# Banded attention followed by a two-layer block: the four VectorE copies that build the attention masks stand in slot 10 of the loop and not in slot 1

## Chip, cores and metric

The kernel runs on one core of a Trainium2 chip. The metric is the device time of one execution in microseconds (us); less is better. The engines are named as in the profile: PE is TensorE (its weight loads are PEld), DVE is VectorE, ACT is ScalarE, POOL is GpSimd, SP is SyncE.

## What is computed

Attention with 8 batches, 8 heads, 576 positions and 64 dimensions a head, in which a position sees only those at most 32 away, and then a block of two matrix products with a smooth ReLU between them on the 4608 tokens of 512 features:

```python
scores = q @ k.T / 8 ; mask = |pos_i - pos_j| <= 32
attn   = softmax(where(mask, scores, -1e9))
x      = (attn @ v) with the heads side by side        # 4608 x 512
h      = x @ w_in                                      # 4608 x 2048
g      = h if h >= 1 ; 0 if h <= -1 ; (h + 1)**2 / 4 between
out    = g @ w_out                                     # 4608 x 512
```

## The kernel before

**Tiles.** Everything is done in bf16 on PE, with sums in fp32. Tokens go in groups of 256 (`TB`), 18 of them. The first product takes 8 pieces of 256 of the 2048 features for each group, so there are 144 of these steps. Each pass of the big loop (`a` from 0 to 151, called a **slot** here) makes one such step: 8 matmuls of line 463 into a PSUM tile `hp`, then a ReLU on ACT (line 467), a maximum on DVE (line 469) and a minimum with a product on DVE (line 470) that give a piece of `gT`. The tile `hp` has two PSUM banks to rotate through (in slots 6 and 7 one of another pool), and the maximum is the last to read it, so the matmuls of slot `a + 2` need the maximum of slot `a`.

The second product is cut in **quarters** (`quarter`, line 414): 4 matmuls with 4 of the 16 rows of `w_out`. From slot 16 on there is one quarter in a slot, for the group before; the eight quarters of the very first group of tokens are spread over slots 9 to 15 by a list written out by hand: `(9, 0), (11, 4), (12, 1), (13, 5), (13, 2), (14, 6), (15, 3), (15, 7)`. The first number is the slot. Quarters 3 and 7 take the last quarter of `w_out`.

**The attention beside it.** What the attention needs is put between these steps by the table `ev`, also by hand: transposes of q and k on PE with a copy out of PSUM (`tpose`, lines 178 to 181), scores (lines 218 and 243) with an exponential on ACT, the sums over the band (line 284), their reciprocal on ACT and the product that writes `xT` on DVE (lines 296 and 299). Whole numbers run before the slot's quarters, and halves such as 1.5 after them. In slots 1 and 1.5 the transposes of the second half of q and k of batch 0 are made. Each has two parts; the first part is copied out of PSUM by ACT and the second by DVE, and the second part of k uses the PSUM bank that the second part of q was in. From slot 2 to slot 16 all such copies are ACT's.

**The masks.** The band is applied in one of two ways. In slots before 14 a matmul with the identity adds a large negative bias to the scores (`add_mask`, line 197). From slot 14 on DVE multiplies the exponentials by `mask4` or `mask8` (line 192), two bf16 tiles of ones and zeros, 128x1024 and 128x384. They are made once, by four DVE copies that repeat a piece of `band`, two for each half of the partitions (line 475). The first multiplication with a mask comes in slot 19.

**Loads.** All inputs but the first q come by DMAs that POOL issues, in the order of the program: k and v of batch 0, the first quarter of `w_in`, the second half of q and k, the other twelve pieces of `w_in`, then q and k of batch 1 with the first part of `w_out`, two more parts of `w_out`, v of batch 1, and the second half of batch 1 with the last part of `w_out` as its first transfer. Each of POOL's DMAs waits, before it is issued, for the landing of the one that used the same of eight semaphores, so that at most eight are under way. Each engine takes its instructions in the order of the program, which is written by hand (`manual_schedule`).

Of the kernel before, what the change touches and what calls it, by code (L numbers as in the profile page):

```python
# [14 lines left out]
def kernel(  # L15
# [72 lines left out]
    def load_nat(b, t):  # L88
        src, dst, nm = ((q, qn, "qn"), (k, kn, "kn"))[t]
        x = dst[b] = nat.tile([128, NU, 2, D], BF, name=nm, tag=nm)  # L90
        for h in range(2):
            nc.gpsimd.dma_start(out=x[:, :, h], in_=src[b, NY * h:NY * h + NY].rearrange("y s d -> (y s) d")  # L92
                                .rearrange("(u p) d -> p u d", p=128))

    def load_v(b, n):
        if b not in vn:
            vn[b] = nat.tile([128, 2 * NC, 2, D], BF, name="vn", tag="vn", bufs=3)
        h, a = divmod(n, 2)
        y = NY * h + 2 * a
        nc.gpsimd.dma_start(out=vn[b][64 * a:64 * a + 64, :, h], in_=v[b, y:y + 2].rearrange("y s d -> (y s) d")  # L100
                            .rearrange("(c r) d -> r c d", r=64))
# [81 lines left out]
    def xpose(b, t):  # L183

        nc.sync.dma_start_transpose(out=qkT(b, t).rearrange("d (u p) -> d u p", p=128),
                                    in_=(qn, kn)[t][b].rearrange("p u h d -> p (u h d)"))
# [115 lines left out]
    def flush():  # L302
        while muls:
            muls.pop(0)()
# [93 lines left out]
    for b in range(LONG, B):  # L398
        a = sl[5 * (b - 1) - 7] - 17
# [7 lines left out]
    def quarter(x):  # L407

        tt, ff = divmod(x, 4)
        if tt not in op:  # L410
            op[tt] = ps_o.tile([128, DM], FP, name="op", tag="op"), []
        o, done = op[tt]
        for j in range(4 * ff, 4 * ff + 4):
            nc.tensor.matmul(o, gT[tt // 2][:, j, 128 * (tt % 2):128 * (tt % 2) + 128], w_out[:, j],  # L414
                             start=not done, stop=len(done) == 2 * NF - 1, skip_group_check=True)
            done.append(j)
        if len(done) == 2 * NF:
            osb = osp.tile([128, DM], FP, name="osb")
            A.copy(osb, o)  # L419
            nc.sync.dma_start(out=out[128 * tt:128 * tt + 128, :], in_=osb)  # L420

    def run(pos):
        todo = []
        for fn, *x in ev.get(pos, []):
            if fn is sums:
                todo.append(sums(*x))
            elif fn is tpose:
                part = x.pop()
                todo.append(tpose(*x, (A.copy, V.tensor_copy)[part if pos < 2 or pos > 16 else 0], tp1((ps_s, ps_n)[part])))
                if part:  # L430
                    while todo:
                        todo.pop(0)()
            elif fn is keep_warm:
                keep_warm(*x)
            else:
                pool = (x.pop(),) if x[-1] in (ps_s, ps_n, ps_o) else ()
                fn(*x, eng, *pool)
        for end in todo:
            end()

    for a in range(NF * NB + NF):
        t, f = divmod(a, NF)
        eng = None if a < 14 else V
        post = [x for n, x in quarters if n == a] if a < 2 * NF else [a - NF]
        for b, x in loads.get(a, []):
            if x < 2:
                load_nat(b, x)
            else:
                for n in range(4):
                    load_v(b, n)  # L450
        if a == 0 or a > 3:
            flush()
        if t < NB:
            if t not in gT:
                gT[t] = gtp.tile([128, 2 * NF, TB], BF, name="gT", tag="gT")
            r0 = TB * t % RING
            if a in (6, 7):
                hp = ps_o.tile([128, 2, TB], FP, name="hp", tag="op")
            else:
                hp = ps_h.tile([128, 2, TB], FP, name="hp", tag="hp")  # L460
            for j in range(2):
                for n, kk in enumerate((0, 2, 1, 3)):
                    nc.tensor.matmul(hp[:, j], w_in[:, kk, 256 * f + 128 * j:256 * f + 128 * j + 128],  # L463
                                     xT[:, kk, r0:r0 + TB], start=n == 0, stop=n == 3)

            rr = ewp.tile([128, 2, TB], FP, name="rr")
            A.activation(rr, hp, AF.Relu, scale=0.5, bias=0.5)  # L467
            mx = ewp.tile([128, 2, TB], FP, name="mx")
            V.tensor_max(mx, hp, rr)  # L469
            V.scalar_tensor_tensor(gT[t][:, 2 * f:2 * f + 2], rr, 1.0, mx, op0=ALU.min, op1=ALU.mult)  # L470
        flush()
        if a == 1:
            for h in range(2):
                for m, n, w in ((mask4, 8, 128), (mask8, 4, TAIL)):
                    V.tensor_copy(m[HD[h]].rearrange("p (n j) -> p n j", n=n), band[HD[h], 64 * h:64 * h + w]
                                  .rearrange("p (n j) -> p n j", n=1).to_broadcast([64, n, w]))
        run(a)
        for x in post:
            quarter(x)
        run(a + 0.5)  # L480
        for x in xps.get(a, []):
            xpose(*x)
# [30 lines left out]
```

The softmax here doesn't subtract the row's maximum and nothing guards it: scores larger than these inputs give would overflow.

## Time and profile before

| | |
|---|---|
| four runs | 320.50, 320.57, 321.77, 321.84 us; median 321.17 |
| the profiled execution | 320.5 us, of which the profile's span is 318.4 and 2.1 lie around it |
| PE busy | 305.7 us (96% of the span) |
| DVE busy | 248.9 us (78%) |
| ACT busy | 193.5 us (61%) |
| POOL busy | 88.7 us (28%) |
| granted TensorE clock | 0.998 of full speed |

The profile is of one execution. Times in it count from the start of the span. A row of the timeline has the start, the duration, the engine, the line, the operation, what is written and read with its size, the number of instructions merged in the row, and in brackets the idle time of the engine before it with what ended that. A DMA's row on POOL is the issue alone; the landing is later, and the trace has its time by the semaphore that it raises.

### The profile page before, as it was taken

How to read it: one execution, taken by the hardware profiler on the slowest of the kernel's cores; microseconds unless marked ns; L12 is line 12 of the kernel's file. 1: busy time of each engine (PE TensorE's matmuls, PEld its weight loads, DVE VectorE, ACT ScalarE, POOL GpSimd, SP SyncE). 2: the span in 40 equal slices, each digit the busy share in tenths (PEclk: the TensorE clock that was granted, in tenths of full speed). 3: DMA queues.
4: the chain of work that ended last, by engine and by line, in shares of the span. 5: the costliest groups of instructions: out<-in, count | busy, mean ns of one | idle time of the engine just before them, and what ended most of it. 6: DMA issues, size and time to landing. Idle time of an engine off the chain costs nothing.

```text
span 318.4 us, 8557 instructions
## 1 busy us (share of the span) xinstructions
PE 305.7 (96%) x3651; PEld 201.8 (63%) x3651; DVE 248.9 (78%) x390; ACT 193.5 (61%) x318; POOL 88.7 (28%) x121
## 2 busy tenths in 40 slices
PE   8968998999999999999999999999999999999995
PEld 3546665666666666666666666666666666667652
DVE  3278956787888888888888888888888888878760
ACT  3649656675775676666766666566676666554421
POOL 8795937896403706040502100000000000000000
PEclk9999999999999999999999999999999999999999
DMA  9999999999999999959991955005410010100111
GB/s 145 164 129 186 150 175 159 198 141 163 169 140 129 165 179 194 150 63 115 183 147 38 106 118 100 35 35 108 102 43 35 33 35 35 36 33 35 51 48 66
DMA packets 122661, 34.52 MB, mean 108 GB/s; under 512 B 108800, under 2 KB 117760, under 8 KB 122624
## 3 DMA queue, kind: packets, MB, share of 16 engines
q0 software_dynamic: 93760, 18.06, 73.0%
q1 hardware_dynamic: 28864, 15.93, 22.3%
q8 instruction: 28, 0.46, 0.6%
q14 instruction: 9, 0.07, 0.1%
HBM read 36.70 MB, written 9.44 MB: 145 GB/s over the span
## 4 chain that ended last, share of the span: by engine, by line
PE 79%; DMA 8%; POOL 7%; DVE 3%; ACT 2%; issue 1%; POOLq 0%; ACTq 0%
PE op L414 37%; PE hp L463 34%; DMA w_out<-in_moe_w_out_dram 6%; PE bb L284 5%; POOL w_in L104 3%; POOL vn L100 2%; DMA w_in<-in_moe_w_in_dram 2%; PE bb L218 2%; POOL kn L84 1%; DVE gT L470 1%; DVE mx L469 1%; PE tp L178 1%; ACT rr L467 1%; POOL w_out L108 0%; DVE pt L192 0%
## 5 line engine op out<-in xcount | busy, mean ns | idle before, releaser
L463 PE MATMUL hp<-xT,w_in 128*128 128x256 bf16 x1152 | 149.2, 273 | 0.7 <-DVE xT L299 0.5
L414 PE MATMUL op<-w_out,gT 128*128 128x512 bf16 x576 | 146.5, 380 | 1.3 <-DMA w_out<-in_moe_w_out_dram 1.3
L467 ACT ACTIVATE rr<-hp 128x512 f32<-128x512 f32 x144 | 85.8, 596 | 90.2 <-PE hp L463 88.8
L463 PEld LDWEIGHTS <-w_in 128*128 128x128 bf16 x1152 | 111.5, 98 | 41.7 <-issue 1.1
L469 DVE TENSOR_TENSOR mx<-hp,rr 128x512 f32<-128x512 f32 x144 | 99.3, 690 | 38.0 <-ACT rr L467 36.0
L470 DVE SCALAR_TENSOR_TENSOR gT<-rr,mx 128x512 bf16<-128x512 f32 x144 | 99.6, 692 | 4.9
L414 PEld LDWEIGHTS <-gT 128*128 128x128 bf16 x576 | 53.5, 98 | 42.8 <-issue 1.3
L226 ACT ACTIVATE pt<-bb 128x1024 bf16<-128x1024 f32 (+1 forms) x33 | 33.2, 1012 | 6.3 <-PE bb L218 5.1
L100 POOL DMA_DIRECT2D vn<-in_v_dram x32 | 27.6, 888 | 26.8 <-PE bb L218 26.3
L296 DVE TENSOR_TENSOR xT<-bb,rc 128x512 bf16<-128x512 f32 (+1 forms) x32 | 21.1, 658 | 10.8 <-ACT rc L291 10.2
L419 ACT COPY osb<-op 128x512 f32<-128x512 f32 x36 | 21.0, 582 | 12.1 <-PE op L414 11.7
L291 ACT ACTIVATE rc<-lr 128x512 f32<-128x512 f32 (+2 forms) x40 | 23.5, 587 | 1.3
L92 POOL DMA_DIRECT2D qn<-in_q_dram x10 | 12.3, 1242 | 39.2 <-DMA qT<-qn 38.7
L290 ACT ACTIVATE lr<-bb 128x512 f32<-128x512 f32 (+2 forms) x40 | 22.0, 550 | 1.1 <-PE bb L284 1.0
L284 PE MATMUL bb<-pt,ones 64*64 64x256 bf16 (+3 forms) x352 | 19.5, 255 | 1.2 <-DVE xT L296 0.6
L192 DVE TENSOR_TENSOR pt<-pt,mask 128x1024 bf16<-128x1024 bf16 (+1 forms) x33 | 20.3, 614 | 0.2 <-ACT pt L226 0.2
L284 PE MATMUL bb<-pt,vn 64*64 64x128 bf16 (+3 forms) x712 | 18.4, 204 | 1.0 <-issue 1.0
L284 PEld LDWEIGHTS <-vn 64*64 64x64 bf16 x712 | 16.7, 107 | 1.1 <-issue 1.1
L284 PEld LDWEIGHTS <-ones 64*64 64x64 bf16 x352 | 10.2, 105 | 9.8 <-issue 9.0
L84 POOL DMA_DIRECT2D kn<-in_k_dram x24 | 13.0, 549 | 9.6 <-DMA w_out<-in_moe_w_out_dram 4.1
L92 POOL DMA_DIRECT2D kn<-in_k_dram x10 | 12.1, 1224 | 6.0 <-DMA kT<-kn 3.0
L218 PE MATMUL bb<-qT,kT 64*64 64x128 bf16 x520 | 13.0, 217 | 0.8 <-DVE kT L181 0.8
(44 smaller groups left out, 102.9 us busy)
## 6 DMA issues: line engine op xcount, KB each, us to landing
out_dram<-osb SPq DMA_DIRECT2D x36, 256.0 KB, 2.3
vn<-in_v_dram POOLq DMA_DIRECT2D x32, 144.0 KB, 7.9
qn<-in_q_dram POOLq DMA_DIRECT2D x10, 288.0 KB, 8.0
kn<-in_k_dram POOLq DMA_DIRECT2D x10, 288.0 KB, 9.0
w_in<-in_moe_w_in_dram POOLq DMA_DIRECT2D x16, 128.0 KB, 5.0
w_out<-in_moe_w_out_dram POOLq DMA_DIRECT2D x4, 512.0 KB, 8.8
kn<-in_k_dram POOLq DMA_DIRECT2D x24, 72.0 KB, 4.5
qn<-in_q_dram POOLq DMA_DIRECT2D x20, 72.0 KB, 5.6
```

Source lines behind the costliest of these rows:

```text
L92: nc.gpsimd.dma_start(out=x[:, :, h], in_=src[b, NY * h:NY * h + NY].rearrange("y s d -> (y s) d") .rearrange("(u p) d -> p u d", p=128))
L100: nc.gpsimd.dma_start(out=vn[b][64 * a:64 * a + 64, :, h], in_=v[b, y:y + 2].rearrange("y s d -> (y s) d") .rearrange("(c r) d -> r c d", ...
L226: A.activation(p, ps[:, :, :128 * n].rearrange(like, y=m), AF.Exp, scale=D ** -0.5)
L284: nc.tensor.matmul(bb[HD[h], a, o + c0:o + c1], ones[HD[a]] if c is None else vn[b][HD[a], c, h], p(a, h), start=n == 0, stop=True, skip_g ...
L290: A.activation(lr[:, :, :D0], bb[:, :, D0:2 * D0], AF.Ln)
L291: A.activation(rc[:, :, :D0], lr[:, :, :D0], AF.Exp, scale=-1.0)
L296: muls.append(lambda: V.tensor_mul(o, bb[:, :, :D0], rc[:, :, :D0]))
L414: nc.tensor.matmul(o, gT[tt // 2][:, j, 128 * (tt % 2):128 * (tt % 2) + 128], w_out[:, j], start=not done, stop=len(done) == 2 * NF - 1, s ...
L463: nc.tensor.matmul(hp[:, j], w_in[:, kk, 256 * f + 128 * j:256 * f + 128 * j + 128], xT[:, kk, r0:r0 + TB], start=n == 0, stop=n == 3)
L467: A.activation(rr, hp, AF.Relu, scale=0.5, bias=0.5)
L469: V.tensor_max(mx, hp, rr)
L470: V.scalar_tensor_tensor(gT[t][:, 2 * f:2 * f + 2], rr, 1.0, mx, op0=ALU.min, op1=ALU.mult)
```

## The change

```diff
@@ -469,7 +469,7 @@
             V.tensor_max(mx, hp, rr)
             V.scalar_tensor_tensor(gT[t][:, 2 * f:2 * f + 2], rr, 1.0, mx, op0=ALU.min, op1=ALU.mult)
         flush()
-        if a == 1:
+        if a == 10:
             for h in range(2):
                 for m, n, w in ((mask4, 8, 128), (mask8, 4, TAIL)):
                     V.tensor_copy(m[HD[h]].rearrange("p (n j) -> p n j", n=n), band[HD[h], 64 * h:64 * h + w]
```

On DVE the same 390 instructions stand in another order: the four copies, which stood between the last product of slot 1 and the two copies of the transposes of slots 1 and 1.5, stand now after the last product of slot 10 and before the maximum of slot 11. That is 23 instructions further on: two copies out of PSUM, the nine pairs of slots 2 to 10 and three products that write `xT`. The order on PE, ACT, POOL and SP is unchanged, and no instruction waits for anything else than before. All four copies are still ahead of the first multiplication with a mask (slot 19).

## Prediction

> **What bounds the kernel now.** I read the page first. PE is busy for 305.7 of 318.4 us, so only the few places where PE stands still can be gained or lost. The list of what PE waited for (times from 17 to 50 us) has four rows:
>
> ```profile
> PE tp L178 <- DVE qT L181: 2.5, 1, 2.5
> PE op L414 <- DMA w_out<-in_moe_w_out_dram: 1.3, 1, 1.3
> PE bb L284 <- issue: 1.0, 1, 1.0
> PE hp L463 <- DVE xT L299: 0.5, 1, 0.5
> ```
>
> Each row has the waiting and the releasing instruction, the sum in us, how often, and the longest. The first looks like the place of this change: PE waits 2.5 us for a DVE copy out of PSUM. The second comes later in time. DVE's and then PE's timeline show the first:
>
> ```profile
> 18.69 0.69 DVE L470 SCALAR_TENSOR_TENSOR gT<-rr,mx 128x512 bf16<-128x512 f32 x1
> 19.30 1.38 DVE L475 COPY mask<-band 64x1024 bf16<-64x1024 bf16 x4
> 20.72 0.72 DVE L181 COPY qT<-tp 128x512 bf16<-128x512 bf16 x1
> ```
>
> ```profile
> 21.48 0.41 PE L178 MATMUL tp<-ident,kn 128*64 128x128 bf16 x8 [2.52 <-DVE qT L181]
> ```
>
> The four mask copies stand right ahead of the copy of qT, whose PSUM bank PE needs. Of PE's 2.52 us, 1.42 (20.72 - 19.30) are theirs. A reader who stops here forecasts 1.4 us of gain. But the chain of work that ended last, up to 50 us, doesn't pass through that wait at all:
>
> ```profile
> 16.27 7.43 POOL w_in L104 x12
> 23.70 0.13 issue
> 23.84 8.31 DMA w_out<-in_moe_w_out_dram
> 32.15 0.28 issue
> 32.43 0.53 POOL kn L84
> 32.96 1.51 POOL w_out L108 x2
> 34.48 3.36 POOL vn L100 x4
> 37.84 11.43 DMA w_out<-in_moe_w_out_dram
> 49.26 0.04 issue
> 49.30 0.38 PE op L414
> ```
>
> From 16 to 49 us it is a chain of loads and their issues. It ends with the last quarter of w_out, which lands at 49.26; PE had been ready for it at 49.30 - 1.29 = 48.01. Behind 49.3 the chain is PE's almost throughout. So the start of PE's long busy stretch is set by that landing, and what PE wins before it is waited away there.
>
> **The change part by part.**
>
> *What goes from slot 1.* Four copies, 1.38 us of DVE, 1.42 from start to start. The copy of qT then starts at about 19.30, PE's second part of k at 20.06 and no longer at 21.48, and the matmuls of slot 2 could start at 20.41 and no longer at 21.83. They need the third piece of w_in, whose two halves land at 20.24 and 20.90 in the trace. So PE gains 21.83 - 20.90 = 0.9 us there, not 1.4. The next pieces bind less: they land at 22.53, 24.23, 26.80, 28.12 and 29.51, against starts of 23.54, 25.49, 28.16, 29.55 and 30.42. PE's lead of some 0.9 us is thus kept up to slot 9. It is cut at the transposes of batch 1 (last q at 34.03, PE at 34.68: 0.65 left) and at quarter 2 (third part of w_out at 43.05, PE's fifth matmul of that row at 43.53: 0.48 left). PE would come to the last quarter of w_out at 48.01 - 0.48 = 47.5 and wait 1.7 us, not 1.29. Worth at the end: nothing, if the landing stays.
>
> *What comes to slot 10.* The same four copies, 1.38 us, behind the last product of slot 10. That one ends at 38.56 before, and earlier by at most what DVE won in slot 1; the copies end by 39.94 at the latest. Queued behind them on DVE is the maximum of slot 11, which began at 38.80: late by at most 1.14. It frees the bank for the matmuls of slot 13, which began at 41.78; the late maximum ends at 40.63. Of slot 11's part of gT the first reader is a quarter of slot 17, after 52 us. DVE stood idle for 0.24 + 0.92 + 0.99 us before the maxima of slots 11 to 13 and catches up there. Cost: nothing, hidden by these idle times; without them 1.4. No DMA is issued by the copies, and the masks' first reader starts at 60.78.
>
> *What the move does to the loads.* This is the part the trace doesn't settle. POOL's twelve issues of w_in (16.27 to 23.70) run beside the copies. One of them, which spans 19.88 to 20.62, took 0.747 us, the other eleven 0.63 to 0.68. And the transfers slow down just then; the table by windows (the last two columns are the share of DMA engines and GB/s):
>
> ```profile
> 18.50:19.40 0.90, 0.46 (x11) 0.35 (x11) 0.87 (x3) 0.40 (x1) 0.90 (x3) 1.00 1.30 174
> 19.40:20.30 0.90, 0.00 (x0) 0.00 (x0) 0.89 (x3) 0.35 (x1) 0.90 (x2) 1.00 0.90 87
> 20.30:21.20 0.90, 0.00 (x0) 0.00 (x0) 0.87 (x3) 0.00 (x0) 0.90 (x2) 1.00 1.22 158
> ```
>
> Against the mean of 174 and 158 the hole is worth 0.9 x (166 - 87) / 166 = 0.43 us of transfers. From there to 32.15 the loads stand in one unbroken queue, and the issues from 32.43 on wait for the landing at 32.15, so that 0.43 us would arrive at 49.26 in full if the copies made the hole. The other end is 0: the hole can be the queue running dry for another reason, for there is a larger one from 34.4 to 35.9 us with no such copy near. The row is nearer to neither; I take the middle, 0.2 us of gain. In the new place the same hole costs nothing: at 37 to 39 us a second part, a third part of w_out and four loads of v are still in the queue, 7 us and more of work ahead of the last part.
>
> The Trainium skill speaks against the new place: "SBUF — State Buffer", section "Who interferes with whom", says that a VectorE copy in a two-port mode holds the port pair it shares with GpSimd for the whole instruction, and that GpSimd, which writes the descriptors of its own DMAs, is blocked until then. By it the last part of w_out, issued at 37.84, would meet the copies, up to 1.38 us late. The row speaks for a touch only (0.747 against 0.68).
>
> **Sum.** 0 (slot 1, waited away at 49.3) + 0 (slot 10) - 0.2 (loads) = -0.2 us. Against the profiled execution that is 320.5 - 0.2 = 320.3; it was among the two faster of four runs. From their median 321.17 it gives 321.0.
>
> **The rivals.**
>
> *The loads come forward by more.* If the copies had kept POOL's descriptors back for all of their 1.38 us, the landing could come forward by up to that, and PE would be ready for it (47.5). Against it: the issue beside them lost 0.1 us and the hole is worth 0.43. I price it between, -0.9: 320.3.
>
> *Slower: an instruction fetch falls into the first part of w_out.* The trace has 16 KB packets of the instruction queue, about one for 256 instructions of PE, each some 0.9 us on one DMA engine. One at 25.48 to 26.44 goes with a landing 1.9 us after the one before, where the neighbours have 0.7. The next, at 31.61 to 32.50, starts when the first part of w_out (landed 32.15) is all but through. If PE is 0.9 us ahead, that fetch comes near 30.7, in the middle of that transfer. Each landing needs all 16 engines, so it is late by up to 0.9, and with it the chain from 32.15. That decides once the fetch moves by more than some 0.5. Price +0.9: 322.1. Against it: the 0.43 above is in hand, and the fetch need not follow PE.
>
> *Slower: the copies hold the last part of w_out.* At most the copies' own 1.38: 322.6. It decides only if the queue ahead is shorter than the delay; it is 7 us.
>
> *The first glance is right: 1.4 us of gain, 319.8.* It needs a landing at 47.9, which nothing here moves so far. That PE's matmuls wait for a late maximum in slots 12 to 15 would have to cost over 1.29 + 0.48 before it shows.
>
> **How the numbers follow.** Forecast (between -0.4 and +0.3, so 320.8 to 321.5): 0.60. Loads forward by more: 0.12. Fetch: 0.15. Last part of w_out held: 0.05. Full gain: 0.03. Something that the trace doesn't show, on the slower side: 0.05. The four runs lie 0.67 to either side of their median, which widens each end. The range is 319.6 to 322.6. A measurement of this kernel can tell 0.5% (1.6 us) from no change: below 319.56 I give 0.05, above 322.78 0.08, between 0.87.
>
> **What would show it.** In the changed profile PE's wait for the copy of qT should be near 1.1 us, not 2.52, the matmuls of slot 2 should start at about 20.9, and PE's wait for w_out should grow to about 1.7 with a landing at 48.8 to 49.3. DVE's copies should stand at 37 to 39 us with no wait of PE for DVE behind them up to 49. The rate between 19.4 and 20.3 us says whether the hole was the copies'. I am wrong if the landing moves by over half a microsecond, or if another wait than w_out's ends last before PE's long stretch.

## The result and the profile after

The changed kernel takes 320.41 us (median of 40 runs, 319.12 to 322.52), the kernel before 321.63 (66 runs, 320.18 to 323.11). The ratio is 0.9967, with a 95% interval of 0.9957 to 0.9977: by the ratio a gain of 0.0033 x 321.63 = 1.06 us, where 0.2 had been forecast. The time lies inside the range, which is wide, but outside the 320.8 to 321.5 of the forecast itself, and the gain is five times the sum. The profiled execution after took 321.48 us (span 319.3), a long one of its kernel, and the one before 320.50, a short one of its own. The two traces side by side thus show the mechanism and not the sign of the change.

What PE waited for after the change, from 17 to 56 us:

```profile
PE op L414 <- DMA w_out<-in_moe_w_out_dram: 1.9, 1, 1.9
PE tp L178 <- DVE qT L181: 1.2, 1, 1.2
PE hp L463 <- DVE xT L299: 0.9, 1, 0.9
PE hp L463 <- DMA w_in<-in_moe_w_in_dram: 0.3, 1, 0.3
```

The stop behind the copy of qT is down from 2.5 to 1.2 us, and the one at the last part of w_out is up from 1.3 to 1.9. DVE's timeline shows the copies in their new place, with nothing ahead of qT's copy in the old one:

```profile
18.93 0.69 DVE L470 SCALAR_TENSOR_TENSOR gT<-rr,mx 128x512 bf16<-128x512 f32 x1
19.54 0.71 DVE L181 COPY qT<-tp 128x512 bf16<-128x512 bf16 x1
...
37.12 1.77 DVE L475 COPY mask<-band 64x1024 bf16<-64x1024 bf16 x4
38.93 0.69 DVE L469 TENSOR_TENSOR mx<-hp,rr 128x512 f32<-128x512 f32 x1
```

PE has no wait for DVE behind them up to 49 us. The end of the load chain, and what PE does then:

```profile
37.38 11.14 DMA w_out<-in_moe_w_out_dram
48.52 0.04 issue
48.56 3.08 PE op L414 x8
```

The eight matmuls took 1.89 us before and 3.08 here. The table by windows says why (its last three columns are the granted TensorE clock, the share of the DMA engines and GB/s):

```profile
46.70:48.50 1.80, 0.00 (x0) 0.00 (x0) 1.74 (x3) 1.71 (x4) 0.01 (x1) 1.00 1.21 198
48.50:49.10 0.60, 0.54 (x3) 0.29 (x3) 0.35 (x1) 0.22 (x1) 0.30 (x1) 1.00 1.28 227
49.10:52.50 3.40, 3.40 (x12) 1.47 (x10) 0.27 (x1) 1.17 (x2) 3.40 (x6) 0.50 0.98 91
52.50:54.00 1.50, 1.50 (x11) 0.97 (x10) 0.33 (x1) 0.60 (x1) 1.50 (x3) 1.00 1.22 270
```

PE is idle for 1.8 us in the first row, and soon after it the clock stands at half for 3.41 us (49.10 to 52.51 in the trace). Such a stretch costs about half its length, 1.7 us, and leaves a mark on the mean clock of a run: 0.5 x 3.41 / 318 = 0.005. That makes it countable without a trace. I call a run **low** whose mean clock is at most 0.9955; the listed clocks are 0.995 and less or 0.997 and more, none between. (The half clock at the very end of a span is under 0.003 of the mean and has no work in it.) Of 41 runs of the changed kernel, 8 are low; they average 322.09 us and the other 33 average 320.17. A mean says that a run had such a stretch and not where it was.

### The profile page after: what moved, and what is told of

Same layout as the page of the kernel before. It is cut to its first block, busy times and chain, and to the rows that moved or that the text cites. A ratio compares the mean times of both kernels' runs of the same rounds, so it can differ in the third digit from the quotient of the medians.

```text
span 319.3 us, 8557 instructions
## 1 busy us (share of the span) xinstructions
PE 306.7 (96%) x3651; PEld 201.9 (63%) x3651; DVE 249.4 (78%) x390; ACT 193.5 (61%) x318; POOL 88.7 (28%) x121
## 4 chain that ended last, share of the span: by engine, by line
PE 79%; DMA 8%; POOL 7%; DVE 3%; ACT 2%; issue 1%; POOLq 0%; ACTq 0%
PE op L414 37%; PE hp L463 34%; DMA w_out<-in_moe_w_out_dram 6%; PE bb L284 5%; POOL w_in L104 3%; POOL vn L100 2%; DMA w_in<-in_moe_w_in_dram 2%; PE bb L218 2%; POOL kn L84 1%; DVE gT L470 1%; DVE mx L469 1%; PE tp L178 1%; ACT rr L467 1%; POOL w_out L108 0%; DVE pt L192 0%
```

## The experiments

The theories: **clock** (the stop in slot 1 lets the clock fall), **hold** (it matters that PE is held in slot 1, by whatever means), **load** (the copies disturb the loads that POOL issues at 19 to 21 us). "Place" is what slot 10 itself may cost. The ratio is to the kernel before on the same chip.

| kernel | median us (runs) | low runs | ratio and interval |
|---|---|---|---|
| before, all whose clock is listed (the 12 of "before again" among them) | 321.49 (99) | 70 | |
| changed | 320.41 (40; clock of 41) | 8 | 0.9967, 0.9957 to 0.9977 |
| before again | 321.60 (12) | 10 | 1.0012, 0.9994 to 1.0030 |
| copies in slot 17 | 321.79 (12) | 4 | 1.0009, 0.9987 to 1.0031 |
| changed + memsets in slot 1 | 320.98 (12) | 7 | 0.9978, 0.9960 to 0.9996 |
| copies in slot 1 behind kT | 320.03 (6) | 0 | 0.9947, 0.9931 to 0.9963 |
| the same again | 319.86 (6) | 1 | 0.9953, 0.9934 to 0.9972 |
| before + ten matmuls in slot 1.5 | 320.72 (12) | 0 | 0.9985, 0.9965 to 1.0006 |
| the same again | 320.42 (11) | 0 | 0.9972, 0.9957 to 0.9987 |
| changed + memsets + ten matmuls | 320.40 (12) | 1 | 0.9971, 0.9951 to 0.9991 |
| changed + seven matmuls in slot 15 | 320.35 (12) | 0 | 0.9967, 0.9949 to 0.9984 |
| behind kT + five and seven matmuls | 320.70 (12) | 0 | 0.9980, 0.9965 to 0.9995 |
| before without the wait at 49 us | 321.42 (12) | 9 | 0.9997, 0.9979 to 1.0016 |
| changed without that wait | 319.45 (8) | 0 | 0.9946, 0.9925 to 0.9966 |

A time is the profile's span and 2.1 us around it. In the kernels with memsets or with five or ten matmuls in slot 1 that isn't so in every run: with memsets it is 1.7 to 1.8 us in most, and in 12 of the 59 runs of these five sets it is 2.5 to 3.5. Where that matters the spans are compared below.

**Before again.** No edit.

> The kernel before, unchanged, to see the granted clock of each of its runs and a second trace. Its runs so far heap up near 320.5 and near 321.7 us. Clock theory: the 2.5 us for which PE stands still at 19 to 21.5 us lets the clock drop to half for one stretch of 3.4 us in most executions, so the runs near 321.7 have a mean clock some 0.005 lower than those near 320.5, and the trace has such a stretch between 19 and 30 us. Hold and load theories: the clock is alike in both heaps (0.998 or 1.0), and the two differ by when the last part of w_out lands. The ratio to the kernel before is 1.000 either way.

The clock theory holds. Low runs are 10 of 12 here, and 70 of 99 with those that ran beside the experiments; the low ones average 321.73 us and the others 320.72, though five of the others lie at 321.3 to 321.5. This trace, of a low run of 322.76 us, has the stretch (windows, then PE's timeline):

```profile
20.00:23.00 3.00, 0.07 (x5) 0.06 (x4) 2.84 (x6) 0.76 (x1) 3.00 (x6) 0.99 1.22 133
23.00:26.30 3.30, 3.30 (x40) 2.10 (x43) 0.96 (x2) 0.60 (x1) 2.70 (x5) 0.50 1.30 155
26.30:29.60 3.30, 3.30 (x88) 2.52 (x84) 2.27 (x4) 3.16 (x6) 2.07 (x5) 1.00 1.38 188
```

```profile
22.93 0.64 PE L178 MATMUL tp<-ident,kn 128*64 128x128 bf16 x8 [2.92 <-DVE qT L181]
23.51 1.89 PE L463 MATMUL hp<-xT,w_in 128*128 128x256 bf16 x8
...
50.67 1.90 PE L414 MATMUL op<-w_out,gT 128*128 128x512 bf16 x7
52.61 0.38 PE L463 MATMUL hp<-xT,w_in 128*128 128x256 bf16 x2
53.51 0.81 PE L463 MATMUL hp<-xT,w_in 128*128 128x256 bf16 x6 [0.52 <-DVE xT L296]
```

The eight matmuls of slot 2 take 1.89 us where they took 1.05. And at 50.67 there is no wait: the last part of w_out had landed at 50.03, so here PE is late, not the load. (PE had also lost 1.17 us in this run to a late load of v, at 12.5.) The trace with memsets in slot 1, below, is low too: PE comes at 49.48 to a load that landed at 49.28. From there to the end of the span both take 269.97 us, against 269.08 to 269.17 in the eight traces at full clock in which PE starts there on the load's landing. So a late PE loses 0.9 us behind slot 15 as well, where it waits for the product that writes xT (0.52).

The Trainium skill, "TensorE: Matmul & The Clock Gate", Part 1, describes a gate that halves the clock and judges by free-running windows of 3.4 us. The stretches here, 3.41 us at 0.50, agree in length and depth. The same page, "Why this matters for your kernels", warns of gaps over about 3 us; here less is enough.

The traces show how much. By the record of the granted clock in each of the fourteen, it changes only a whole number of times 3.413 us after it first rises (17.07, 44.37 and 310.61 us are 5, 13 and 91 times that). Cut into such pieces, what counts is PE's idle time in the piece before. It is 1.90 to 2.91 us before each piece at half clock that follows a stop in the work (after 1.90, slot 17 2.08, memsets 2.07, before again 2.91), and never above 1.63 before a piece at full clock. In the first trace of before, at full clock, a boundary at 19.93 cuts the stop of 2.52 us in two, and the pieces hold 1.02 and 1.56 us of idle time (a row has the piece, its length, then PE's busy time; the granted clock is third from the end):

```profile
16.51:19.93 3.42, 2.40 (x36) 1.29 (x34) 3.22 (x6) 2.12 (x4) 3.42 (x7) 1.00 0.94 108
19.93:23.34 3.41, 1.85 (x40) 1.38 (x43) 2.18 (x5) 0.42 (x1) 3.41 (x7) 1.00 1.23 148
23.34:26.76 3.42, 3.42 (x100) 2.63 (x91) 2.62 (x4) 3.42 (x7) 2.20 (x4) 1.00 1.30 162
```

This is why the same stop drops the clock in some executions only. If a boundary can fall anywhere, a stop of 2.52 us puts more than a limit of 1.63 to 1.90 us into one piece in 0.78 to 0.62 of the executions (2.52 + 3.41 less twice the limit, over 3.41); that is an estimate, and 70 of 99 is 0.71.

**Copies in slot 17** (against the kernel before):

```diff
-        if a == 1:
+        if a == 17:
```

> The copies stand in slot 17, behind the landing of the last part of w_out, where DVE has idle time. If only leaving slot 1 counts, the time is that of the changed kernel: ratio 0.9967 to the kernel before (0.9957 to 0.9977). If the copies in slot 10 disturb the loads issued at 37 to 39 us, this kernel is faster than the changed one by up to 1.4 us: ratio about 0.993. If the copies in slot 17 hold up PE (DVE's idle time there is 2 us in the slot before), slower by up to 1.4: ratio about 1.001.

It is as slow as before, though only 4 of 12 runs are low: the other 8 average 321.20. The expectation's last case is met. DVE's row and then PE's:

```profile
56.67 1.61 DVE L475 COPY mask<-band 64x1024 bf16<-64x1024 bf16 x4
```

```profile
59.09 0.41 PE L178 MATMUL tp<-ident,kn 128*64 128x128 bf16 x8 [0.69 <-DVE qT L181]
61.26 0.42 PE L218 MATMUL bb<-qT,kT 64*64 64x128 bf16 x16 [0.78 <-ACT rr L467]
```

From slot 17 on half of the copies out of PSUM are DVE's again, and the mask copies stand ahead of one, as in slot 1. There is no load behind which PE's wait could hide there: 0.69 + 0.78, less the 0.39 that the changed kernel waits at that place, is 1.1 us. That is the loss: from the start of slot 15's quarters to the end this trace takes 270.23 us, 1.1 more than 269.1, and the 8 runs that aren't low average 1.03 us more than those of the changed kernel. Leaving slot 1 is thus not enough; slot 10 is a place where PE waits for no copy of DVE's.

The trace is of a low run, and its half clock falls at 21.93, behind slot 1, though no mask copy stands there. PE stood still for 0.87 us behind qT's copy and, 0.4 us of matmuls later, for 1.21 us behind a load of w_in, both in one piece:

```profile
18.51:21.93 3.42, 1.34 (x23) 0.93 (x22) 2.12 (x4) 0.75 (x1) 3.42 (x7) 1.00 1.13 135
21.93:25.34 3.41, 3.41 (x44) 2.19 (x43) 1.39 (x2) 1.67 (x3) 3.06 (x6) 0.50 1.28 165
```

So short stops add up. PE still waited 1.2 us for w_out later: a low run doesn't have to make PE late.

**Changed, with memsets in slot 1** (against the changed kernel; `idle` is a new tile of 128x640 f32):

```diff
+        if a == 1:
+            for _ in range(2):
+                V.memset(idle, 0.0)
         if a == 10:
```

> The changed kernel with two DVE memsets of 128x640 fp32 (about 0.68 us each, 1.4 together) where the copies had stood in slot 1. They write a tile that nobody reads and read nothing. Hold theory (what counts is that PE stands still for 1.4 us more in slot 1): the gain is gone, ratio 1.000 (0.998 to 1.002), PE's wait for the copy of qT about 2.5 us again. Load theory (what counts is that the copies meet POOL's issues of w_in): the gain stays, ratio 0.997. Half of each: 0.9985.

PE's wait is back (2.6 us), low runs are back (7 of 12), and by the ratio about a third of the gain is gone; it lies between the two theories and excludes neither 0.997 nor 0.998. But 0.35 us of what is left lie outside the span (1.77 us there, not 2.12). The mean span is 319.05, against 319.32 before and 318.43 in the changed kernel: inside the span 0.6 of the 0.9 us are gone, which is nearer to the hold theory.

**Copies behind kT** (against the kernel before):

```diff
         flush()
+        run(a)
+        for x in post:
+            quarter(x)
+        run(a + 0.5)
         if a == 1:
...
-        run(a)
-        for x in post:
-            quarter(x)
-        run(a + 0.5)
         for x in xps.get(a, []):
```

> The copies stay at the end of slot 1, but behind the two copies out of PSUM that PE waits for (about 21.5 to 22.9 us on DVE), so PE isn't held while the copies still run beside POOL's issues of w_in. Hold theory: the gain of the changed kernel is there, ratio 0.997 (DVE's late maximum of slot 2 costs nothing by slot 9). Load theory: the gain is gone, ratio 0.999 to 1.001.

> The copies at the end of slot 1 behind the copies out of PSUM, once more, for more runs and their clocks. Hold theory: as the changed kernel, ratio 0.9967 (0.994 to 0.998), with at most one run in four under a clock of 0.9955, from the wait at the last part of w_out. If the place in slot 10 cost something that this place does not: ratio 0.995 again and no run with a low clock.

Both times the gain is there in full, with the copies still in slot 1 and at 21.4 to 22.9 us. PE's stop is 1.2 us in both traces, and 1 run of 12 is low. This excludes the load theory's 0.999 to 1.001 for this place. The intervals of both reach into that of the changed kernel, so that it beats the change isn't shown.

**Before, with matmuls in PE's stop** (against the kernel before; `keep_warm` is the kernel's own helper for matmuls on zeros):

```diff
-    at(1.5, *through(0, 1, 1))
+    part0, part1 = through(0, 1, 1)
+    at(1.5, part0, (keep_warm, 10, ps_o, "op"), part1)
```

> The kernel before, with ten matmuls on a tile of zeros that nobody reads put between the two parts of k's transposes in slot 1.5, where PE stands still for 2.5 us. DVE's order is that of before, so PE is still held until the copy of qT. Clock theory (the stop in slot 1 costs time because it lets the clock fall to half for 3.4 us in about two of three executions): the clock stays at 0.997 or more in nearly all runs and the runs near 321.6 move to those near 320.5; ratio 0.997 (0.995 to 0.998). Theory that the hold itself counts, or that the copies disturb the loads: ratio 1.000 (0.998 to 1.002), or slower by what PE's matmuls add.

> The kernel before with the ten matmuls on zeros in slot 1.5, once more, beside the kernel with memsets on the same chip. Clock theory: no run with a clock under 0.997 again, median 320.4 to 320.9, ratio 0.997 to 0.9985. Load theory: slower than the kernel with memsets by 0.4 to 0.5 us; if the copies don't touch the loads, by less than 0.3.

No low run in 23, with DVE's order that of before. They average 320.73, just what the runs before average that are not low (320.72; by the spans 318.45 and 318.60). So it is the idle time of PE, not the copies as such, that drops the clock.

**Changed, memsets and matmuls** (against the changed kernel; `idle` as above):

```diff
-    at(1.5, *through(0, 1, 1))
+    part0, part1 = through(0, 1, 1)
+    at(1.5, part0, (keep_warm, 10, ps_o, "op"), part1)
...
+        if a == 1:
+            for _ in range(2):
+                V.memset(idle, 0.0)
         if a == 10:
```

> Copies in slot 10, two memsets of 1.4 us together in their old place, and ten matmuls on zeros in PE's stop in slot 1.5. Against the next kernel it differs in what DVE does at 19 to 21 us (memsets, not copies) and in the four copies of slot 10. The clock stays up in both, so PE's way is not slowed and the landing of w_out's last part binds. Load theory (the copies beside POOL's issues of w_in make the loads late): faster than the next kernel by 0.4 to 0.5 us, ratio 0.997 to the kernel before. If the copies don't touch the loads: the same as the next kernel within 0.3 us, ratio 0.998 to 0.9985.

Beside the repeat of the kernel above on the same chip, its median is 320.40 against 320.42. The median spans are 318.1 and 318.3, and 1 run of 12 is low. Whether DVE runs mask copies or memsets while POOL issues w_in makes no difference that these runs can tell; with intervals of 0.5 to 0.6 us to either side they do not exclude 0.4 alone. The traces speak against the load theory more sharply. From the first issue of the long row of w_in (16.27 us before, 15.62 after) to the landing of w_out's last part it takes 32.8 to 33.6 us in the five traces with the mask copies in their old place, and 32.9 to 34.2 in the nine others.

**Changed, with seven matmuls in slot 15** ahead of the wait for w_out (against the changed kernel):

```diff
-    at(15, seq[0][0], (*seq[1][0], ps_s))
+    at(15, seq[0][0], (*seq[1][0], ps_s), (keep_warm, 7, ps_h, "hp"))
```

> The changed kernel with seven such matmuls (1.5 us) in slot 15, ahead of the quarter that waits 1.9 us for the last part of w_out. Clock theory: the one run in five of the changed kernel whose clock falls to 0.993 to 0.995 and that takes 321.5 to 322.5 us is gone; all runs lie at 319 to 321, the median at 320.0, ratio 0.995 to 0.996 to the kernel before. If the matmuls make PE late for the landing: slower by up to 1.5 us, ratio 1.000. If the clock at that place has no weight: ratio 0.9967, as the changed kernel.

PE's timeline shows them in the wait, and the next eight matmuls at full speed:

```profile
46.74 1.68 PE L318 MATMUL z<-warm 128*128 128x512 bf16 x6
48.26 1.89 PE L414 MATMUL op<-w_out,gT 128*128 128x512 bf16 x8
```

The low runs are gone (0 of 12, and 0 of 8 in the last kernel below, which has no such wait), which speaks for this stop as the place of the changed kernel's low runs, but the median isn't clearly better: 320.35 against 320.41, ratio 0.9967. The runs that aren't low reach up to 321.44, as those of the changed kernel do without the matmuls (321.53).

**Behind kT, with five matmuls in slot 1.5 and seven in slot 15** (against the kernel with the copies behind kT):

```diff
-    at(1.5, *through(0, 1, 1))
+    part0, part1 = through(0, 1, 1)
+    at(1.5, part0, (keep_warm, 5, ps_o, "op"), part1)
...
-    at(15, seq[0][0], (*seq[1][0], ps_s))
+    at(15, seq[0][0], (*seq[1][0], ps_s), (keep_warm, 7, ps_h, "hp"))
```

> The copies at the end of slot 1 behind the two copies out of PSUM (as in the run before with that place), five matmuls on zeros in PE's stop in slot 1.5 (1.2 us) and seven in slot 15 ahead of the last part of w_out. Clock theory: no run has a clock under 0.997, and with the hold gone too the runs lie at 319 to 321 with a median of 320.0: ratio 0.995 to 0.996 to the kernel before. If the added matmuls make PE late where the loads land early: 320.4, ratio 0.997.

Also no low run, and 0.8 us slower than without the matmuls (320.70 against 319.86 beside it). By these runs the added matmuls cost more than the low runs that they save, though the intervals of the two ratios touch. Its own trace, at 319.43 us, is the shortest of its 12 runs and doesn't show where.

**Both kernels without the wait at 49 us** (line 414 of each; the matmul's last operand):

```diff
-... w_out[:, j],
+... w_out[:, j - 4 * (x in (3, 7))],
```

> The kernel before, but quarters 3 and 7 take the third part of w_out and not the last, so nothing waits for the last part until slot 19 (the first 256 tokens of the output take the wrong rows of w_out for a quarter of their sum). It shows what PE's way to slot 15 is worth when the landing doesn't bind. Where the clock fell in slot 1 PE comes to slot 15 after the landing anyway and nothing is won; where it did not, 1.3 us. With the clock low in about two of three runs: ratio 0.998 to 0.999. If the landing binds in every run: ratio 0.996.

> The changed kernel with the same cut (quarters 3 and 7 take the third part of w_out; the first 256 tokens of the output take the wrong rows for a quarter of their sum). If PE's lead out of slot 1 is there and only waited away at the landing, this gains 1.9 us on the changed kernel and also loses the low clock behind that wait: 1.06 + 1.9 + 0.3 = 3.3 us below the kernel before, ratio 0.990. If there is no such lead, the gain is as in the kernel before with the cut: ratio 0.995.

Before, nothing is won (0.9997). That excludes the 0.996 of a landing that binds in every run and fits the clock theory: 9 of 12 are low. The three others average 320.27, only 0.45 below those of the kernel before, where 1.3 was expected. After, about 1 us is won on the changed kernel, not 1.9, and by the means 0.4 of it is the low runs that are gone. PE's waits show the one that takes its place:

```profile
PE hp L463 <- DVE xT L296: 0.5, 1, 0.5
```

With the load out of the way PE comes to slot 16 before xT is written. So PE's lead is real, it is waited away at the load, and part of it would be waited away at the next place.

## Why the prediction was right and wrong

*The wait named first is not on the chain; what PE wins in slot 1 is waited away at 49 us.* Right for the profiled execution of before, wrong as a rule, and this is the step that failed. "If the landing stays, nothing" presumed that PE is at slot 15 ahead of the landing. In 70 of 99 runs the clock is low for a while, and in the trace of before run again PE comes 0.6 us after the landing. How late it comes in the other low runs isn't on record; on average they take 1.0 us longer. The trace that I worked from was one of the others (0.998). That the time still lies inside the range is luck as far as the mechanism goes: the range is wide by its rivals and by the scatter of four runs, and no rival names the clock.

*The first stop* was to be 1.1 us and is 1.22; slot 2 was to start near 20.9 and starts at 20.64, where w_in landed earlier too (20.25); the wait at w_out was to be 1.7 and is 1.90. These steps were right, the last by two errors that nearly cancel: PE was ready at 46.66 and not at 47.5, and the load landed at 48.52 and not at 48.8 to 49.3. The landing thus moved by 0.74, over the half microsecond that was to be the sign of being wrong. But the row of w_in was issued 0.65 us earlier in that execution (15.62, not 16.27), ahead of the place of the change, and from there to the landing it took 32.90 us, 32.99 before: 0.1 less.

*Slot 10 costs nothing*: right, though the copies took 1.77 us there and not 1.38. The idle time of slots 11 to 13 took it, and slot 17 shows the price without that cover, 1.1 us.

*The loads, -0.2*: the hole of 87 GB/s is not the copies'. In the trace after it stands at 18.5 to 19.4 us, with no mask copy there:

```profile
18.50:19.40 0.90, 0.58 (x11) 0.36 (x11) 0.87 (x2) 0.28 (x1) 0.90 (x3) 1.00 1.00 87
```

That is 2.9 us behind the first issue of the row of w_in, and it was 3.1 before. The issue of 0.747 us isn't a sure sign of a touch either: in the trace after one takes 0.722 without the copies.

*The rivals.* "The loads come forward by more" had the size (-0.9), but nothing on record shows its mechanism, neither the memsets nor the times to the landing. The instruction fetch does move into the first part of w_out (29.65 after, 31.61 before), and that part then lands 3.10 us after the w_in piece before it (28.60 to 31.70), against 2.64 before (29.51 to 32.15). That is 0.46 more, half of the price of 0.9. Whether the fetch does it is open: in the trace with the copies behind kT one starts at 30.01, inside the same transfer, which ends 2.67 us after the piece before it (28.01 to 30.68). The last part of w_out was not held: 11.1 us from issue to landing, 11.4 before. The full 1.4 was not reached.

*The missing term* is the clock. By the means: low runs cost 1.01 us each before, in 70 of 99 runs, 0.71 on average; after, 1.92 each in 8 of 41, 0.37. That leaves 0.34 us of gain from the clock. The runs that are not low differ by 320.72 - 320.17 = 0.55. Together 0.89, the difference of the means (321.44 and 320.55). The two sets were not taken side by side, and the ratio has 1.06.

**What stays open** is the 0.55, more than half of the gain. Since 269.1 us follow on the start of slot 15's quarters in each of the eight traces named above, it should arise before that start. Taken back from the mean spans of the runs that aren't low, the start lies near 49.5 us before and 49.0 after; that is an estimate. The same reckoning gives 49.35 with ten matmuls, 48.9 with the copies in slot 17 (less its own 1.1), 48.7 behind kT, 49.1 with seven matmuls and 49.4 with five and seven. So it is early where PE isn't held in slot 1 and no matmul is added. Why is not shown: the traces' times from the issue of w_in to the landing don't differ that way, and no trace with a long span at full clock was taken (one of 321.55 us, with memsets and ten matmuls, has a span of 318.1). It may be that instruction fetches follow PE's lead.

## What to carry to other kernels

A stop of PE that lies off the chain can still cost time: it can drop the clock for the next 3.4 us, and then PE, not the load, can arrive last. Stops that lie close together add up. Before costing a stop at nothing, look at the granted clock of several runs, not at one trace. Short work that is needed late goes behind the copies that PE waits for, and into a stretch where no copy out of PSUM on that engine is due; an idle slot by itself isn't enough.

## What was not expected of the hardware

About 1.9 us of idle time in one piece of 3.41 us was enough to halve the clock for the next, in one stop or in two; up to 1.63 us never did it in fourteen traces. How a stop lies against the boundaries decides as well: in the two traces of the kernel before, a stop of 2.92 us dropped the clock and one of 2.52 did not. The four mask copies took 1.19 to 1.77 us in the traces, with the same operands. Matmuls that only keep PE busy left 1 low run in 59, and brought a gain over the same kernel without them only where the stop was 2.5 us or longer.
